# First stage of an attention and two-MoE kernel: the written-out order of its 1002 steps, and the engines of 168 of them, replaced

## The chip, the cores and the metric

The kernel runs on one core of a Trainium2 chip. The metric is device time in microseconds (us) of one launch. Engines are named as the profile names them: PE (TensorE matmul), PEld (TensorE weight load), DVE (VectorE), ACT (ScalarE), POOL (GpSimd), SP (SyncE, which here issues the DMAs of this stage). SBUF is the on-chip working memory and PSUM the memory that matmuls write.

## The reference

Attention over 2 batches, 8 heads, 768 positions, head size 64, each row seeing 8 global keys and the 96 last ones; then a dense mixture of 4 experts, weighted by given probabilities; then a mixture of 8 experts with a capacity of 192 tokens each, chosen by sorting all gate logits.

```python
scores = scale * q @ k.T + bias;  scores = where(keep, scores, -1e9)     # keep: global or local
a = exp(scores - max); a = a / (sum(a) + 1e-9);  x = a @ v               # (1536, 512) after reordering
out1 = sum_e p[:, e] * (relu(x @ w1[e]) @ w2[e])                         # 4 experts, 512 -> 1024 -> 512
out  = routed: relu(out1[mask] @ v1[e]) @ v2[e]                          # 8 experts, 192 tokens each
```

## The kernel before

Every float32 operand is split into a float16 high part and a float16 low part after scaling by a power of two, and each product is made of three float16 matmuls. So next to the matmuls there are many elementwise passes of 128 x 512: one that makes the high part (`hi`), one that subtracts it (`lo`), and so on.

The kernel has several stages. The change touches only the first one (`phase1`), which does the attention for 12 blocks of 128 rows, j = 0 to 11, and for each finished block the first MoE expert (e = 0). Later stages do experts 1 to 3, the routing, and the 8 routed experts; their code is the same in both kernels. The second stage begins with matmuls of expert 1, whose first weight matrix (weights 2) and second one (weights 3) are loaded and split near the end of stage one.

The steps of `phase1` are small closures with names, and a string `ORDER1` lists all 1002 of them in the order in which they are emitted. Each engine has one in-order queue, so the list fixes the order on every engine, on SP's DMA queue too. A token `name.j` is step `name` of block j (without `.j`: 0), and `/V`, `/A`, `/G` puts it on DVE, ACT or POOL; without a suffix it takes the default of `ENGINE`:

```python
ENGINE = dict(whi="G", hi="G", bias="G", keys="V", values="V", ph="G", pl="G", xhi="A", relu="A", hhi="V",
              hlo="G", add="A")
```

The steps of a block, with the line that the profile shows:

- `load` (three DMAs of q, k, v, L552), `sq` (sums of squares, ACT, L561), `run`, `total`, `scale` (power-of-two scales, a dozen tiny DVE instructions, L569 to L599).
- `hi0..2` (L544 on DVE, L540 on ACT, L542 on POOL) and `lo0..2` (DVE, L620: 128 x 512, reads two SBUF tensors); `T0`, `T1` (DMA transposes), `swap` (two DMAs).
- `keys`, `values`, `kglob`, `vglob` rescale the former block's keys and values; `bias` is two instructions, from bf16.
- `qk0..3` (PE, L695), `max0..3` (DVE, L706: reads PSUM and one SBUF tensor), `exp` (ACT, L715), `ph` (copy to f16, `/V /A /G`), `pl` (the rest: L730, DVE or POOL), `PT0`, `PT1` (DMA transposes), `pv` (PE, L753), `x` (three DVE instructions, L762 to L765).
- `norm` (ACT, L778), `rscale`, `xhi`, `xlo` (DVE, L791) and `xT` (DMA transpose, L770), which makes the block ready for the expert.
- `g00..g13` (8 steps of 12 matmuls, L834), `relu0/1`, `hhi0/1` (high part), `hlo0/1` (L1383, DVE or POOL), `y00..y07` (24 matmuls of 512 columns, L845), `add0`.

Weights k = 0 to 3: `wl0.k`, `wl1.k` (two DMAs of 1 MB, L372), `wsq` (ACT, L402), `wsum` (PE, L408), `wsc` (DVE), `whi0..7.k` (any engine), `wlo0..7.k` (DVE, L473). `wl0.3` may start when `wlo0.2` to `wlo3.2` have read their buffer, `wl1.3` after `wlo4.2` to `wlo7.2`. At the end of the old list SP finds `PT1.11`, `xT.10`, `wl0.3`, `xT.11`, `wl1.3` in this order. `check` makes sure that every step comes after those that it depends on.

Of the kernel before, what the change touches and what calls it, by code (L numbers as in the profile page):

```python
# [49 lines left out]
    max0.1 exp0.1 PT0 wlo6 qk1.1 max1.1 pl2 qk2.1 ph3 pl3 PT1 bias1.1 max2.1 qk3.1 sq0.3 max3.1 pv lo2.2 wsq1.1 x  # L50
    ph0.1 pl0.1 wsum.1 sq2.3 T1.2 norm exp1.1 exp2.1 wsc.1 keys.2/G run.3 ph1.1/A both ph2.1/A total.3 T0.2 bias0.2
    whi1.1 rscale scale.3 xhi/V kglob.2 values.1/G load.4 exp3.1 xlo sq1.4 swap.2 xT pl1.1 wlo1.1 PT0.1 hi2.3/V hi1.3
    qk0.2 max0.2 lo1.3 pl2.1 ph3.1/A whi5.1/A pl3.1 qk1.2 sq0.4 lo2.3 wlo4 whi2.1 hi0.3/A vglob.1 g00 pe0 sq2.4
    bias1.2/A exp0.2 max1.2 g01 whi4.1 lo0.3 g02 g03 PT1.1 g10 T1.3 run.4 ph0.2 total.4 T0.3 wlo2.1 g11 qk2.2 pv.1
    scale.4 whi7.1 max2.2 qk3.2 load.5 x.1 swap.3 exp1.2 exp2.2 hi1.4 hi0.4 relu0 keys.3 bias0.3 pl0.2/V max3.2 norm.1
    g12 ph1.2/A ph2.2/V hhi0/A rscale.1 g13 xhi.1 exp3.2 sq1.5 whi3.1 lo0.4 kglob.3 xlo.1 pl2.2 whi0.1 ph3.2 wlo5.1
    sq0.5 lo1.4 T0.4 pl1.2/V qk0.3 xT.1 pl3.2 qk1.3 sq2.5 max0.3 max1.3 relu1 T1.4 qk2.3 values.2 qk3.3 hi2.4/A g00.1
    g01.1 g02.1 wlo0.1 vglob.2 bias1.3/A wlo4.1 PT0.2 keys.4 hhi1/A PT1.2 exp0.3 bias0.4 exp1.3 g03.1 whi6.1 ph0.3/A
    g10.1 run.5 hlo0 swap.4 max2.3 total.5 scale.5 y00 g11.1 y01 hi1.5 pv.2 g12.1 pl0.3/V ph1.3/A hi0.5 hlo1/V lo2.4
    kglob.4 lo0.5 pl1.3/V relu0.1 wl0.2 exp2.3 y02 x.2 qk0.4 g13.1 max3.3 norm.2 bias1.4 ph2.3/V wlo3.1 rscale.2  # L60
    exp3.3 load.6 xhi.2 PT0.3 sq1.6 hi2.5/V max0.4 xlo.2 qk1.4 ph3.3 lo1.5 wlo6.1 y03 T0.5 xT.2 exp0.4 sq0.6 pl2.3
    sq2.6 y04 max1.4 y05 qk2.4 pl3.3 T1.5 max2.4 qk3.4 values.3/G exp1.4 ph0.4 y06 exp2.4 run.6 keys.5 total.6 vglob.3
    wlo7.1 max3.4 kglob.5 g00.2 bias0.5 g01.2 scale.6 y07 tiles.1 relu1.1/V ph1.4 pl0.4/V pl1.4 g02.2 hi1.6 hhi0.1/A
    swap.5 g03.2 pe0.1 exp3.4 PT1.3 hlo0.1 qk0.5 lo2.5 pv.3 g10.2 hi0.6/A x.3 g11.2 ph2.4/A pl2.4 g12.2 load.7 max0.5
    y00.1 lo0.6 ph3.4/V sq1.7 PT0.4 bias1.5 norm.3 T0.6 rscale.3 qk1.5 pl3.4/V bias0.6 xhi.3/G hhi1.1 exp0.5 max1.5
    hlo1.1 PT1.4 sq0.7 values.4/A sq2.7 g13.2 qk2.5 ph0.5 xlo.3 add0 vglob.4 max2.5 y01.1 lo1.6 y02.1 hi2.6/V run.7
    pe0.2 xT.3 y03.1 y04.1 pl0.5 qk3.5 y05.1 exp1.5 relu0.2/V y06.1 ph1.5 exp2.5 lo2.6 max3.5 swap.6 pv.4 T1.6 y07.1
    ph2.5/A g00.3 total.7 g01.3 x.4 g02.3 pl1.5 relu1.2 scale.7 tiles.2 exp3.5 ph3.5/A hhi0.2 hi1.7/V bias1.6 qk0.6
    pl2.5 g03.3 norm.4 hi0.7/A pl3.5 PT0.5 qk1.6 hlo0.2 rscale.4 g10.3 max0.6 load.8 xhi.4/V hi2.7 g11.3 g12.3 g13.3
    values.5/A y00.2 sq1.8 lo0.7 qk2.6 hhi1.2/A xlo.4 PT1.5 lo1.7 exp0.6 y01.2 relu0.3/V y02.2 sq0.8 max1.6 pe0.3  # L70
    y03.2 T0.7 bias0.7 hlo1.2 ph0.6 y04.2 xT.4 T1.7 sq2.8 y05.2 qk3.6 vglob.5 y06.2 exp1.6 pv.5 y07.2 ph1.6 tiles.3
    max2.6 exp2.6 run.8 lo2.7 keys.7/G relu1.3/V pl0.6/V hhi0.3 load.9 hlo0.3 g00.4 add0.1/V kglob.7 g01.4 g02.4 g03.4
    total.8 g10.4 y00.3 swap.7 hhi1.3/G relu0.4 hlo1.3 g11.4 max3.6 x.5 exp3.6 y01.3 norm.5 ph2.6/V y02.3 pl2.6
    ph3.6/A sq1.9 scale.8 hi1.8 g12.4 qk0.7 y03.3 sq0.9 hi0.8/V qk1.7 pl1.6 y04.3 pl3.6/V lo0.8 rscale.5 xhi.5 bias1.7
    max0.7 g13.4 sq2.9 xlo.5 wl1.2 PT0.6 bias0.8 hi2.8/V max1.7 lo1.8 qk2.7 PT1.6 pe0.4 y05.3 T0.8 xT.5 y06.3 exp0.7
    y07.3 tiles.4 ph0.7 exp1.7 hhi0.4/G qk3.7 hlo0.4 max2.7 pv.6 T1.8 add0.3/V exp2.7 ph1.7 swap.8 add0.2 relu1.4
    lo2.8 y00.4 load.10 max3.7 y01.4 x.6 ph2.7 y02.4 keys.8/A g00.5 g01.5 run.9 exp3.7 y03.4 pl2.7/V total.9 kglob.8
    ph3.7/A g02.5 pl0.7 scale.9 qk0.8 g03.5 max0.8 norm.6 qk1.8 pl1.7 hhi1.4/A rscale.6 sq1.10 PT0.7 bias1.8 pl3.7
    exp0.8 g10.5 hlo1.4 g11.5 hi1.9 values.7 hi0.9/V pe0.5 g12.5 ph0.8 y04.4 lo0.9 qk2.8 g13.5 vglob.7 bias0.9/A
    max1.8 y05.4 sq0.10 y06.4 lo1.9 xhi.6/V relu0.5/V hi2.9/A qk3.8 PT1.7 xlo.6 pl0.8 y07.4 tiles.5 sq2.10 T0.9 exp1.8  # L80
    hhi0.5/G hlo0.5/V pv.7 relu1.5 T1.9 y00.5 keys.9/A max2.8 y01.5 ph1.8 xT.6 exp2.8 run.10 y02.5 hhi1.5/G lo2.9
    hlo1.5 pl1.8 max3.8 y03.5 exp3.8 swap.9 x.7 norm.7 load.11 total.10 y04.5 PT0.8 y05.5 g00.6 ph2.8 ph3.8/A kglob.9
    pl2.8 scale.10 rscale.7 g01.6 y06.5 xhi.7/G qk0.9 pl3.8/V hi1.10/A g02.6 g03.6 max0.9 sq1.11 xlo.7 qk1.9 hi0.10/A
    y07.5 sq0.11 exp0.9 PT1.8 relu0.6/V max1.9 g10.6 tiles.6 hhi0.6/A bias1.9 pe0.6 qk2.9 exp1.9 values.8 xT.7
    bias0.10 lo0.10 g11.6 g12.6 g13.6 hlo0.6 add0.4 ph0.9/V T0.10 vglob.8 qk3.9 sq2.11 max2.9 lo1.10 y00.6 y01.6 pv.8
    g00.7 T1.10 relu1.6 g01.7 exp2.9 run.11 pl0.9 max3.9 hhi1.6/A g02.7 g03.7 swap.10 values.9 keys.10 x.8 exp3.9
    ph1.9 y02.6 pl1.9 ph2.9 kglob.10 total.11 g10.7 hlo1.6 PT0.9 g11.7 g12.7 scale.11 ph3.9/A norm.8 qk0.10 qk1.10
    y03.6 hi2.10/A rscale.8 pl2.9 g13.7 max0.10 pl3.9 qk2.10 hi1.11/A PT1.9 xhi.8 relu0.7 exp0.10 xlo.8 xT.8 bias1.10
    ph0.10 y04.6 y05.6 max1.10 vglob.9 max2.10 y06.6 hi0.11/V hi2.11/V exp1.10 y07.6 pv.9 exp2.10 ph1.10 lo0.11 qk3.10
    tiles.7 hhi0.7 T0.11 max3.10 g00.8 g01.8 relu1.7 lo2.10 lo2.11 lo1.11 pl0.10 ph2.10/A hlo0.7/V pe0.7 values.10/G  # L90
    g02.8 exp3.10 g03.8 hhi1.7 add0.6 g10.8 pl2.10 x.9 add0.5/V T1.11 ph3.10/V g11.8 relu0.8/V g12.8 y00.7 y01.7
    pl1.10 y02.7 hlo1.7 swap.11 close0 keys.11 bias0.11/A y03.7 kglob.11 gate3 y04.7 wsq0.2 y05.7 pe0.8 y06.7 norm.9
    y07.7 qk0.11 rscale.9 PT0.10 wsq1.2 qk1.11 g13.8 max0.11 tiles.8 hhi0.8/A pl3.10 relu1.8/V hlo0.8 max1.11 y00.8
    y01.8 vglob.10 qk2.11 PT1.10 xhi.9 xlo.9 y02.8 bias1.11 y03.8 pv.10 exp0.11 qk3.11 hhi1.8 max2.11 wsum.2 hlo1.8/V
# [1751 lines left out]
```

## Time and profile before

| what | value |
|---|---|
| runs | 895.56, 891.95, 895.22 us, median 895.22 |
| profiled execution | 895.84 us, span 894.1 us |
| mean granted TensorE clock | 0.962 |
| busy in the span | PE 755.8 us, DVE 645.1, ACT 528.1, POOL 334.4 |
| stage one | from the start to 256.46 us, where the first matmul of expert 1 starts |

A span is the time from the first to the last instruction; the profiled execution's own time is 1.7 us longer. A busy time is the sum of an engine's instruction times, without overlaps. An instruction that is held up inside the engine by another engine is busy too, for longer.

### The profile page before, as it was taken

The page shows a single profiled execution, that of the slowest core. Times are in us where ns is not written, and L with a number is a line of the kernel's source. Part 1 is how long each engine was busy: PE and PEld are TensorE (multiplying, and loading weights), DVE is VectorE, ACT ScalarE, POOL GpSimd, SP SyncE. Part 2 cuts the span into 40 slices and gives each one's busy share as a digit, 9 for nine tenths or more (in the row PEclk, how much of TensorE's full clock was granted, in tenths as well). Part 3 has the DMA queues.
Part 4 walks back from the last instruction along what each step waited for, and adds up shares of the span by engine and source line. Part 5 has one row for each costly group of instructions (what it writes and reads, how often), then busy time and mean ns, then how long its engine had stood idle before and what let it go on. Part 6 is the DMA issues. An engine that isn't in the chain of part 4 may idle for free.

```text
span 894.1 us, 19304 instructions
## 1 busy us (share of the span) xinstructions
PE 755.8 (85%) x7539; PEld 544.6 (61%) x7539; DVE 645.1 (72%) x1710; ACT 528.1 (59%) x1046; POOL 334.4 (37%) x403
## 2 busy tenths in 40 slices
...
GB/s 232 217 177 184 178 188 212 151 112 139 154 142 0 108 81 1 95 31 89 1 26 12 14 25 14 36 2 1 59 213 84 131 139 347 247 277 321 193 34 39
DMA packets 196860, 105.20 MB, mean 118 GB/s; under 512 B 167585, under 2 KB 167585, under 8 KB 196769
## 3 DMA queue, kind: packets, MB, share of 16 engines
...
q0 software_dynamic: 2048, 6.34, 3.0%
q8 instruction: 59, 0.97, 0.5%
...
## 4 chain that ended last, share of the span: by engine, by line
PE 41%; DVE 25%; issue 12%; DMA 9%; ACT 7%; POOL 4%; SPq 1%; POOLq 0%; DVEq 0%; ACTq 0%
PE pH L834 16%; PE pY L845 14%; DVE C L967 3%; PE pR L834 2%; PE pY L1012 2%; ACT junk L402 2%; DVE jk L970 2%; DMA xt<-xs 2%; DVE t L706 2%; DMA xk<-in_k_dram 2%; PE pH L1255 2%; DMA xg<-g 2%; DVE w L473 1%; PE pR L1275 1%; POOL out_dram L1291 1%
## 5 line engine op out<-in xcount | busy, mean ns | idle before, releaser
L834 PE MATMUL pH<-xT,w 128*128 128x128 f16 (+2 forms) x2304 | 238.7, 263 | 10.7 <-DMA xT<-xs 9.2
L834 PEld LDWEIGHTS <-w 128*128 128x128 f16 x2592 | 209.0, 100 | 61.8 <-DMA xT<-xs 7.1
L845 PE MATMUL pY<-w,hh 128*128 128x512 f16 x544 | 162.3, 380 | 3.7 <-DVE y L544 1.3
L808 ACT ACTIVATE H<-pH 128x512 f32<-128x512 f32 (+1 forms) x94 | 52.8, 564 | 100.6 <-PE pH L834 75.8
L845 PE MATMUL pY<-w,hl 128*128 128x512 f16 x272 | 103.4, 380 | 4.2 <-POOL hl L1383 3.1
L980 ACT ACTIVATE Cj<-C 128x128 bf16<-128x128 bf16 (+11 forms) x88 | 75.3, 856 | 43.1 <-DVE C L967 42.1
L542 POOL TENSOR_SCALAR hh<-H 128x512 f16<-128x512 f32 x55 | 36.6, 665 | 134.3 <-ACT H L808 123.8
L845 PEld LDWEIGHTS <-hh 128*128 128x128 f16 x544 | 49.9, 98 | 52.9 <-issue 2.6
L1255 PEld LDWEIGHTS <-w 128*128 128x128 f16 x768 | 65.5, 100 | 23.4 <-DMA xg<-g 18.5
L432 DVE SCALAR_TENSOR_TENSOR w<-raw,wsr,w 128x1024 f16<-128x1024 f32 x52 | 65.2, 1278 | 6.3 <-ACT w L540 6.3
L1275 PE MATMUL pR<-hh,w 128*128 128x192 f16 x512 | 67.1, 249 | 0.0
L1255 PE MATMUL pH<-xg,w 128*128 128x192 f16 x528 | 49.8, 254 | 20.2 <-DMA xg<-g 18.3
L803 DVE TENSOR_TENSOR hl<-H,hh 128x384 f16<-128x384 f32 (+1 forms) x56 | 34.6, 617 | 44.2 <-POOL hh L542 43.1
L967 DVE TENSOR_SCALAR C<-LR,Lg 128x1024 bf16<-128x1024 f32 (+7 forms) x88 | 64.1, 729 | 3.1 <-PE pw L986 1.7
L1275 PEld LDWEIGHTS <-w 128*128 128x128 f16 x768 | 64.7, 99 | 2.3 <-issue 2.0
L1275 PE MATMUL pR<-hl,w 128*128 128x192 f16 x256 | 63.8, 249 | 0.0
L1012 PE MATMUL pY<-w,xT 128*128 128x512 f16 x192 | 61.6, 396 | 0.0
L402 ACT ACTIVATE w<-raw 128x2048 f16<-128x2048 f32 x18 | 34.3, 1905 | 42.1 <-PE pY L845 23.4
L715 ACT ACTIVATE t<-t,mx,ec 128x256 f32<-128x256 f32 (+1 forms) x96 | 55.2, 576 | 2.9
L540 ACT ACTIVATE w<-raw,wsr 128x1024 f16<-128x1024 f32 (+1 forms) x49 | 50.7, 1053 | 6.5 <-DVE wsr L302 6.5
L852 DVE SCALAR_TENSOR_TENSOR y<-pY,pe,y 128x512 f32<-128x512 f32 x22 | 16.5, 748 | 51.6 <-PE pY L845 47.0
L695 PE MATMUL pS<-kT,qT 128*128 128x128 f16 x176 | 29.4, 245 | 25.9 <-DVE mx L706 9.9
...
## 6 DMA issues: line engine op xcount, KB each, us to landing
...
pt<-pp SPq DMA_TRANSPOSE x24, 4.9
```

The costliest lines, as they stand in the source:

```text
L402: A.activation(x, s.raws[k, q][0], AF.Square, accum_out=J["ss"][:, q:q + 1])
L432: V.scalar_tensor_tensor(l, r[:, d2], sc, h, op0=OP.mult, op1=OP.subtract)
L540: s.nc.scalar.activation(out, x, AF.Copy, scale=sc)
L715: s.nc.scalar.activation(t[:, o + hh], t[:, o + hh], AF.Exp, bias=mx[:, 1, hh:hh + 1], scale=e[:, 0:1], accum_out=s.SU[j][:, 2 * g + hh:2 ...
L808: s.nc.scalar.activation(H, ps, AF.Relu, scale=HS)
L834: nc.tensor.matmul(o[f], w[:, d, 128 * (f0 + f):128 * (f0 + f) + 128], x[:, :, c], start=(d == 0 and i == 0), stop=(d == 3 and i == 2))
L845: nc.tensor.matmul(py, l[:, f], w[:, f], start=(f == 0 and i == 0), stop=(f == 7 and i == 2))
L967: V.tensor_scalar(C[:, 8 * i:8 * i + n], x[:, :n, e], l, None, op0=OP.is_ge)
L980: s.nc.scalar.activation(x, C, AF.Copy, accum_out=s.AC[j][:, 1, e:e + 1])
L1012: nc.tensor.matmul(py, a[:, f], w[:, f], start=(n == 0), stop=(n == 23))
L1255: nc.tensor.matmul(ps[0][:, f % 2], w[:, d, 128 * f:128 * f + 128], xg[:, :, c], start=(k == 0), stop=(k == 11))
L1275: nc.tensor.matmul(ps[0][:, d % 2], w[:, f, 128 * d:128 * d + 128], h[:, f], start=(k == 0), stop=(k == 23))
```

## The change

Only `ORDER1` changes: the same 1002 steps, in another order, with 168 of them on another engine. No function changes. How many steps of each kind lie on an engine, before and after:

| step | DVE | ACT | POOL |
|---|---|---|---|
| whi | 4, 8 | 11, 10 | 17, 14 |
| hi | 10, 4 | 12, 13 | 14, 19 |
| bias | 0, 1 | 5, 11 | 19, 12 |
| keys | 5, 6 | 3, 0 | 2, 4 |
| values | 4, 4 | 3, 1 | 3, 5 |
| ph | 8, 11 | 17, 18 | 23, 19 |
| pl | 16, 16 | 0, 0 | 32, 32 |
| xhi | 4, 3 | 5, 6 | 3, 3 |
| relu | 12, 10 | 12, 14 | 0, 0 |
| hhi | 9, 7 | 8, 9 | 7, 8 |
| hlo | 7, 12 | 0, 0 | 17, 12 |
| add | 5, 5 | 7, 7 | 0, 0 |

The start and the end of the two lists (the middle is of the same make):

```diff
-    load sq1 sq0 sq2 wl0 run wl1 route total scale wsq0 hi1/V load.1 hi0/A wsq1 lo1 lo0 hi2 sq1.1 lo2 wsum wsc gate0
-    whi5 sq0.1 whi1/A whi3/V sq2.1 gate1 whi2/V wlo5 gate2 T0 T1 whi4/A run.1 load.2 total.1 wlo3 whi7/A swap tiles
...
-    ph0.11/A exp1.11 y04.8 exp2.11 pl0.11/V ph1.11 max3.11 xT.9 y05.8 ph2.11/V pl1.11/V y06.8 pl2.11/V y07.8 g00.9
-    g01.9 x.10 exp3.11 ph3.11/A pl3.11/V norm.10 tiles.9 add0.7/V g02.9 g03.9 g10.9 g11.9 g12.9 relu0.9/V PT0.11
-    rscale.10 hhi0.9/G hlo0.9/V pe0.9 g13.9 xhi.10/G y00.9 relu1.9/V values.11/A xlo.10 vglob.11 hhi1.9 wsc.2 y01.9
-    y02.9 PT1.11 hlo1.9 y03.9 whi2.2 pv.11 y04.9 whi7.2/V y05.9 whi6.2 whi0.2/A whi1.2 y06.9 xT.10 whi3.2/A whi5.2
-    y07.9 g00.10 x.11 whi4.2 wlo0.2 norm.11 wlo6.2 tiles.10 g01.10 pe0.10 rscale.11 xhi.11/V g02.10 xlo.11 g03.10
-    relu0.10/V g10.10 g11.10 add0.9 hhi0.10/G wlo5.2 g12.10 add0.8/V wlo1.2 wlo3.2 wlo2.2 g13.10 wlo7.2 wlo4.2 close1
-    wl0.3 relu1.10/V xT.11 wsq0.3 hlo0.10 wl1.3 y00.10 y01.10 y02.10 y03.10 g00.11 g01.11 g02.11 wsq1.3 hhi1.10 g03.11
-    g10.11 hlo1.10/V y04.10 wsum.3 y05.10 wsc.3 y06.10 y07.10 g11.11 g12.11 g13.11 relu0.11 whi2.3 tiles.11 wlo2.3
...
+    load wl0 wl1 sq1 sq0 sq2 run total scale hi1/V gate0 load.1 wsq0 wsq1 hi0/V hi2 wsum gate1 lo1 lo0 lo2 sq1.1 T0 T1
+    sq0.1 sq2.1 wsc wl0.1 gate2 whi7/V whi5/V swap wlo7 bias0 whi6/V run.1 total.1 whi2/A qk0 wlo6 scale.1 hi1.1/V
...
+    qk2.11 max2.11 xT.9 hlo1.8 exp0.11 y03.8 exp1.11 pv.10 x.10 y04.8 whi6.2/V g00.9 whi0.2/V qk3.11 values.11/G g01.9
+    norm.10 max3.11 g02.9 g03.9 y05.8 g10.9 rscale.10 whi4.2 exp2.11 xhi.10 ph0.11 y06.8 vglob.11 g11.9 ph2.11/A
+    relu0.9 whi7.2/A pe0.9 xlo.10 y07.8 ph1.11 tiles.9 exp3.11 xT.10 ph3.11/A whi2.2/A pl0.11/V add0.7/V hhi0.9
+    hlo0.9/V g12.9 g13.9 y00.9 relu1.9 y01.9 g00.10 pe0.10 pl1.11 hhi1.9 g01.10 hlo1.9/V y02.9 pl2.11/V y03.9 y04.9
+    PT0.11 y05.9 y06.9 y07.9 pl3.11 wlo6.2 wlo0.2 PT1.11 whi5.2/A g02.10 add0.8 whi3.2/V wlo5.2 g03.10 wlo2.2 add0.9
+    wlo4.2 tiles.10 wlo1.2 pv.11 wlo7.2 g10.10 close1 wlo3.2 g11.10 g12.10 relu0.10/V hhi0.10/G x.11 g13.10 norm.11
+    wl0.3 hlo0.10 rscale.11 relu1.10 wsq0.3 wl1.3 xhi.11/V xlo.11 hhi1.10/G hlo1.10/V xT.11 y00.10 wsq1.3 pe0.11
+    y01.10 y02.10 y03.10 y04.10 y05.10 y06.10 y07.10 wsum.3 wsc.3 g00.11 g01.11 whi3.3 g02.11 whi4.3/V whi5.3 g03.11
...
```

In the middle, SP's queue differs in one thing of size: `wl0.2` stands behind `swap.4` in the old list and behind `swap.10` in the new one, `wl1.2` behind `swap.7` and now behind `swap.11`.

## Rows read from the trace of the kernel before

**Rows 1.** Busy time by stretch (us, then each engine's busy us and count, clock, DMA).

```profile
16.24:215.70 199.46, 146.47 (x1956) 114.06 (x1956) 186.45 (x541) 156.48 (x413) 132.12 (x140) 0.97 0.93 175
215.70:224.90 9.20, 9.20 (x137) 6.98 (x135) 8.02 (x21) 2.62 (x5) 4.88 (x6) 1.00 0.86 125
224.90:256.46 31.56, 24.75 (x248) 17.90 (x247) 18.21 (x35) 9.41 (x14) 8.87 (x10) 0.89 0.44 143
...
100.00:215.70 115.70, 104.68 (x1446) 78.63 (x1444) 110.92 (x319) 92.48 (x240) 79.34 (x83) 1.00 0.87 162
...
241.10:246.50 5.40, 5.40 (x61) 5.40 (x62) 0.00 (x0) 3.68 (x6) 0.00 (x0) 0.60 1.05 386
```

**Rows 2.** DVE's instructions by line in stage one: ns minimum/median/maximum, first and last start.

```profile
L620 DVE SCALAR_TENSOR_TENSOR kn<-xk,asr,kn x12: 739/1184/1665, 10.0 to 197.9; 128x512 f16<-128x512 f32 x12
...
L574 DVE CAST ssb<-ssr x11: 171/173/1152, 18.0 to 180.6; 128x3 bf16<-128x3 f32 x11
...
L706 DVE CUSTOM_DVE_ANT_0 t<-pS,t x96: 271/414/425, 25.4 to 212.1; 128x256 f32<-128x256 f32 x80, 128x128 f32<-128x128 f32 x16
...
L544 DVE TENSOR_SCALAR hh<-H x8: 408/417/836, 107.3 to 236.0; 128x512 f16<-128x512 f32 x8
...
L1383 DVE TENSOR_TENSOR hl<-H,hh x6: 675/691/1092, 82.0 to 236.4; 128x512 f16<-128x512 f32 x6
```

**Rows 3.** DVE in order of time, 89 to 95 us (start, us).

```profile
91.03 1.64 DVE L620 SCALAR_TENSOR_TENSOR kn<-xk,asr,kn 128x512 f16<-128x512 f32 x1
92.60 1.60 DVE L473 SCALAR_TENSOR_TENSOR w<-y,wsr,w 128x512 f16<-128x512 f32 x1
```

**Rows 4.** POOL in order of time, the same stretch.

```profile
89.41 2.72 POOL L730 TENSOR_TENSOR pp<-t,pp 128x512 f16<-128x512 f32 x2
92.11 1.55 POOL L542 TENSOR_SCALAR vs<-vs,ratio 128x1024 f16<-128x1024 f16 x1
```

**Rows 5.** POOL's instructions by line in stage one: ns minimum/median/maximum.

```profile
L542 POOL TENSOR_SCALAR t<-bias,ec x38: 477/695/1452, 22.4 to 207.5; 128x512 f32<-128x512 bf16 x32, 128x256 f32<-128x256 bf16 x6
...
L542 POOL TENSOR_SCALAR kn<-xk,asr x6: 695/699/859, 51.7 to 154.7; 128x512 f16<-128x512 f32 x6
...
L542 POOL TENSOR_SCALAR vs<-vs,ratio x3: 1116/1117/1553, 47.2 to 194.8; 128x1024 f16<-128x1024 f16 x3
...
L1383 POOL TENSOR_TENSOR hl<-H,hh x16: 1151/1160/1585, 74.7 to 231.0; 128x512 f16<-128x512 f32 x16
```

**Rows 6.** DVE in order of time, 224 to 235 us.

```profile
224.21 0.69 DVE L765 TENSOR_TENSOR x<-pO,rs 128x512 f32<-128x512 f32 x1
224.82 2.00 DVE L473 SCALAR_TENSOR_TENSOR w<-raw,wsr,w 128x512 f16<-128x512 f32 x2
...
228.39 0.75 DVE L791 SCALAR_TENSOR_TENSOR xs<-x,rsr,xs 128x512 f16<-128x512 f32 x1
...
230.98 4.34 DVE L473 SCALAR_TENSOR_TENSOR w<-raw,wsr,w 128x512 f16<-128x512 f32 x5
```

**Rows 7.** What SP's queue waited for, 221 to 236 us (us, times, longest).

```profile
SPq L372 <- DVE w L473: 11.8, 1, 11.8
```

**Rows 8.** The chain that ended last, 222 to 262 us (start, us).

```profile
234.60 6.45 DMA xT<-xs
241.10 5.56 PE pH L834 x60
...
251.28 5.18 PE pY L845 x24
```

**Rows 9.** PE in order of time: block 10's g, undisturbed.

```profile
226.00 5.52 PE L834 MATMUL pH<-xT,w 128*128 128x128 f16 x96
```

**Rows 10.** Line 770: issue to landing of the xT transposes, all 12.

```profile
DMA to landing us min/median/max: 3.2/3.6/4.1
```

**Rows 11.** ACT in order of time: the two squares of weights 3.

```profile
240.10 1.91 ACT L402 ACTIVATE w<-raw 128x2048 f16<-128x2048 f32 x1 [13.21 <-DMA raw<-in_moe_w_dram]
...
243.80 1.91 ACT L402 ACTIVATE w<-raw 128x2048 f16<-128x2048 f32 x1 [1.69 <-DMA raw<-in_moe_w_dram]
```

More of the change, by code (lines that the diff above doesn't have):

```diff
@@ L50 @@
[L50 to L94, printed above, removed]
@@ new lines @@
+    qk1.1 lo1.2 wsum.1 wsc.1 exp0.1 qk2.1 T0.2 max1.1 qk3.1 sq1.3 ph3 sq0.3 max2.1 pl3 T1.2 whi6.1 PT1 ph0.1/V both
+    sq2.3 run.3 lo2.2 total.3 max3.1 scale.3 exp1.1 pv whi0.1 whi2.1 exp2.1 bias0.2/A pl0.1 ph1.1 hi1.3 keys.2 probs
+    swap.2 tiles kglob.2 x ph2.1/A lo1.3 exp3.1 ph3.1/A qk0.2 hi0.3/V load.4 max0.2 norm pl1.1 qk1.2 pl2.1 lo0.3
+    bias1.2 consts sq1.4 qk2.2 rscale hi2.3 pl3.1/V max1.2 values.1/G PT0.1 exp0.2 wlo2.1 qk3.2 T1.3 sq0.4 sq2.4
+    whi7.1/A max2.2 xhi/G run.4 xlo ph0.2 exp1.2 total.4 T0.3 whi1.1 exp2.2 ph1.2/A scale.4 lo2.3 vglob.1 PT1.1
@@ new lines @@
+    hi1.4/A max3.2 pv.1 xT hi2.4/A wlo6.1 swap.3 keys.3/G pe0 pl0.2 hi0.4 ph2.2/A bias0.3/A g00 load.5 kglob.3 x.1
+    norm.1 lo1.4 pl1.2 PT0.2 wlo1.1 g01 qk0.3 rscale.1 qk1.3 exp3.2 lo0.4 whi5.1 sq1.5 ph3.2/A g02 values.2 max0.3
+    pl2.2 g03 vglob.2 xhi.1/V sq0.5 pl3.2 g10 g11 g12 qk2.3 sq2.5 max1.3 T0.4 wlo0.1 whi4.1 qk3.3 run.5 exp0.3 xlo.1
+    bias1.3/A lo2.4 total.5 T1.4 ph0.3 g13 scale.5 bias0.4 keys.4 exp1.3 max2.3 PT1.2 hi1.5/A max3.3 hi0.5 pl0.3 pv.2
+    ph1.3/A lo1.5 kglob.4 swap.4 relu1 qk0.4 exp2.3 xT.1 load.6 qk1.4 relu0/V exp3.3 max0.4 g00.1 lo0.5 g01.1 g02.1
```

47 lines of the change are left out of this document (41 added, 6 removed).

## The prediction

> **What bounds the kernel now.** I read the busy shares by slice first (VectorE is at nine tenths or more through most of the first quarter), then the busy time by stretch, then DVE's instructions by line, then the chain that ended last over the end of the stage, and last SP's waits there. Stage one falls into three stretches [rows 1]: A, from 16.24 us, when the first weight scale is known, to 215.70, when DVE has finished the last `pl` (`pl3.11`); B, to 224.90, when `x.11` ends; C, to 256.46, when expert 1 starts.
>
> In A the DVE is busy 186.5 of 199.5 us: it sets the pace. But much of this is not its own work. A `lo` takes 0.74 us at the least and 1.18 in the median, up to 1.67; a copy of three numbers takes 0.17 or up to 1.15; `max`, with one of its tensors in PSUM, never varies (0.425 at the most for the wide form) [rows 2]. Two slow ones in a row, 1.64 and 1.60 us, stand beside POOL instructions that follow each other without a gap and are long too [rows 3, 4]: the two engines take turns. From the start of one to that of the next these DVE instructions are 1.57 us apart, the length of one POOL instruction and one `lo` together.
>
> How much of A is such waiting: I took each form of DVE instruction at its least duration ([rows 2] has the first and four more of some sixty), less the 0.08 us by which it begins before the one before it ends (91.03 plus 1.64 against 92.60 [rows 3]), times its number in the list up to `pl3.11`. That gives 140 us, of which 4 lie before A. So 186.5 - 136 = 50 us of A are waits for POOL. POOL's own work up to there, counted in the same way ([rows 5] has four of its forms), is 113 us: it costs the DVE 50/113 = 0.44 us per us.
>
> In C the engines wait for one thing. `xlo.11` ends at 229.14 [rows 6], but its transpose is issued at 234.60, because SP's queue stands at `wl0.3`, whose buffer the `wlo.2` steps on DVE still read: SP waits 11.8 us for them [rows 7], the last row of them starts at 230.98 [rows 6]. The transpose then takes 6.45 us [rows 8] against 3.6 in the median and 4.1 for the slowest of the twelve that the line's view tells of [rows 10]; the load of 1 MB issued just before it is the only thing new beside it. PE stands still until 241.10, and after that idle time its granted clock is 0.60 [rows 1], between its two levels: 60 matmuls take the time to 246.5, 5.4 us, where 96 took 5.52 at full clock [rows 9]. That is about 2 us lost.
>
> **The change, part by part.** No instruction is added or taken away; the sums are changes of engine and place.
>
> *A, DVE's own work.* Counting tokens up to `pl3.11`, DVE has 22 instructions more in the new list: six `hlo` (0.68 each, 4.1), one `xlo` (0.74), one `add` (0.74), four more of the short scaling kind (eleven for `whi`, `ph`, `bias`, `keys` and `hhi` more, seven for `hi` and `xhi` fewer; 0.42 each [rows 2], 1.7), nine tiny ones of 0.15 (by the cast of three numbers [rows 2]) and a `vglob` (together 1.8). That is 9.1, less 0.08 of overlap for the thirteen larger ones: plus 8. Most were in stretch B before; they come earlier.
>
> *A, POOL's work.* Fourteen `bias` instructions fewer (0.695, -9.3, some narrower), four `hlo` fewer (1.15, -4.6), four `ph` fewer (0.62 by the narrow `hhi` kind, -2.4); five `hi` more (+3.5), two `keys` and two `values` more (1.12 each, +4.5), two small ones (+1.3) [rows 5]. Sum -7: 106 us.
>
> *A, the turns.* At the old rate the new list has 106 x 0.44 = 47 us of waiting, 3 less. That is the upper end, if the new layout does not place POOL's work better. The lower end: the DVE's forms that never waited (`max`, `x`, the reads of PSUM in `relu` and `add`) hold about 50 us in A (`max` alone 80 x 0.41 and 16 x 0.28, 37 [rows 2]; `x`, `relu` and `add` some 20 pieces of the 0.69 of `x` [rows 6]), its idle time is 13, and some 0.13 us of each of 131 POOL instructions hide in the turn itself (start to start 1.57 us [rows 3], where a 0.66 `lo` and a 1.12 `values` would make 1.78 in a row); if POOL filled all of that, 106 - 50 - 13 - 17 = 26 us remain. Both queues are in order and wait for other engines too, so a plan is met only in part; I take 42, a quarter of the way down. A comes out at +8 - 8 = 0, with ends of +5 and -16.
>
> The Trainium skill ("SBUF — State Buffer", "Who interferes with whom") has a rule that speaks against a gain here: the ports that DVE and GpSimd share are an exclusive lock, and the one that comes second waits out the first one's whole instruction. Taken strictly nothing hides in a turn, the 17 us fall away, the least waiting is 106 - 50 - 13 = 43 us, A is +1 at the best and the sum 886. The turns of 1.57 us where the two instructions are 1.78 in a row show that here a part does hide.
>
> *A, PE's cover.* Before the end of `pv.11` the new list has PE do 5.2 us more (four `y` steps at 0.65, four `g` steps at 0.67 [rows 8, 9]). Between 100 and 215.7 us PE has 115.7 - 104.7 = 11 us idle [rows 1] and B has none. So 0 for A and B together needs half of that idle time gone, and A and B can't shrink by more than 6 however well the turns go, unless PE is ahead at 100 us already. It is not: the first `xT` comes about 7 us of DVE work later than before, and the PE work in front of `pv.3` is 3 us less.
>
> *B.* Its length is that of a transpose (`PT1.11`) and `pv.11`; in the new list the eight `wlo.2` (0.66 each from start to start, 5.3 us) lie in it where the work moved to A stood. 0. If that cover were gone, 5.3.
>
> *C.* Now SP has `wl0.3`, `wl1.3`, `xT.11` in this order, and all of `wlo.2` ends before `x.11`. Counting from the end of `x.11` (t): `wl0.3` and `wl1.3` are issued about t - 2. In the old tail the first load was squared 5.9 us after its issue (234.2 to 240.1), the second 9.6 us after the first's issue (243.8) [rows 11]; so the second is squared from t + 7.6 and `wsum.3`, which stands in PE's queue before `g00.11` in the new list, can run at t + 7.6 + 2.1 + 0.4 = t + 10. `xlo.11` ends at t + 3 (it was 4.2 with two `wlo` of 2.00 between [rows 6]); its transpose has two loads before it, lands with the second or 2 us later, and so at t + 8 to t + 10. I take `g00.11` at t + 10 (it was t + 16.2). Then 5.4 us of `g` [rows 9] and 5.2 of `y` [rows 8]. PE has `g10..g13.10` and all of `y.10`, 7.9 us, to fill from `pv.11` to t + 6.5: it idles some 3.5 us where it was 6.6, and I charge half of the clock loss, 1. C lasts 10 + 5.4 + 5.2 + 1 = 21.6 us where it was 31.6: -10. Ends: -12.5 (no clock loss, loads as fast as the first) and -6 (the second load lands 4 us later).
>
> *Moved past queues.* `wl0.2` and `wl1.2` leave the middle for the last blocks; there they go before `PT`, `T` and `xT` of blocks 9 to 11. I cost this at 0, hidden by the PE backlog of that stretch (9.2 of 9.2 busy [rows 1]); a rival below has its price. The later stages keep their code, and their first stretch is PE's, so what stage one gives passes on whole.
>
> Sum: 0 + 0 - 10. Against the profiled execution's 895.84 us this is 885.8; the median of the runs is 0.6 lower, so **885**.
>
> **The rivals.** 0.5% of the time, 4.5 us, is about what a measurement can tell here.
>
> *The turns are as frequent as before* (the change doesn't do what it says). A is +5, C still -10: 890. For it: the list orders each engine but not the engines against each other, and the start of POOL's instructions hangs on ACT and DMA. Against: POOL has 7 us less to do.
>
> *The turns fall much, and PE is the cap.* A and B together -6, C -10: 879. For it: POOL's `bias` work goes to ACT, which has 43 us idle in A [rows 1]. Against: PE would have to run A's last 115 us without a gap.
>
> *Slower: the weight loads move into DMA's busy part.* The DMA engines are at 0.93 in A [rows 1], and one load of 1 MB before a transpose cost 2.9 us (6.45 against 3.6). Two loads now stand in front of blocks 10 and 11, with `wsq1.2` close behind `wl1.2` in ACT's queue, in front of `exp.11`. If the transposes of two blocks (`T`, `PT`) each lose 3 us and ACT waits 4 for the load, A is +5 + 6 + 4 = +15, and with the second load late C gives only 6: +9, 904. It decides from the point where PE has no backlog in blocks 10 and 11. Against: PE was busy for all of B [rows 1], so it had a backlog there.
>
> *The tail gives half.* `wsum.3` in front of `g00.11` waits for a late second load, C -6, and A +2 from the PE work ahead: 891.
>
> **How the numbers follow.** Forecast 0.38 (own range 881 to 889), same turns 0.24, PE cap 0.16, slower 0.11, half tail 0.11. Faster by over 0.5% (under 890.7): 0.38 + 0.16 and two thirds of the second, 0.16: 0.70. Slower: 0.11. Same: 0.19. The range takes in the cap, and the slower case in part: 874 to 899.
>
> **What would show it.** DVE's `lo` median near 0.75 to 1.0 instead of 1.18, and POOL's busy time down by over 7 us. A over by 214 to 218 us on DVE. No SP wait of 10 us on `wlo` before `xT.11`; PE's gap before `g.11` under 4 us; expert 1 starting near 246. Wrong would be: the same medians with PE's gaps longer in the last blocks (turns), an ACT wait on a raw load of several us before `exp.11` (slower rival), or a start of expert 1 after 252.

## The result, and the profile after

The changed kernel takes **880.5 us** (median of 4 runs, 878.84 to 883.16) against 895.39 us before (4 runs, 891.95 to 896.15). The ratio of the runs is 0.9855, with a 95% interval of 0.9818 to 0.9893 (the two medians alone make 0.983): faster by 1.5%. The profiled execution took 880.59 us, with a span of 878.8 us.

Busy time by stretch after (stretch, length, then busy us and count of PE, PEld, DVE, ACT and POOL, granted clock, DMA share, GB/s). Stretch A ends with the later of the last two `pl`; that is now `pl2.11`, on DVE (`pl3.11`, on POOL, ends at 210.1).

```profile
15.60:211.75 196.15, 151.44 (x2052) 120.20 (x2052) 186.94 (x564) 164.17 (x431) 120.22 (x126) 0.98 0.98 181
211.75:219.18 7.43, 7.43 (x109) 5.31 (x107) 7.27 (x14) 0.69 (x1) 0.96 (x2) 1.00 0.63 133
219.18:241.00 21.82, 19.31 (x181) 13.50 (x178) 9.03 (x20) 8.08 (x12) 7.42 (x9) 0.92 0.65 194
100.00:211.75 111.75, 104.77 (x1431) 79.58 (x1429) 107.98 (x324) 93.55 (x247) 68.91 (x70) 1.00 0.91 170
```

Beside [rows 1]: A and B together end at 219.18 instead of 224.90 (-5.7), C lasts 21.82 us instead of 31.40 (-9.6), and expert 1 starts 15.3 us earlier. Both are read from the first matmul of expert 1, which before starts at 256.30; the 256.46 above is where the matmul ahead of it ends:

```profile
256.30 1.89 PE L834 MATMUL pH<-xT,w 128*128 128x512 f16 x8
```

This lead stays to the end: the span is 15.3 us shorter.

DVE's `lo`, its copies of three numbers and the steps beside them, by line (ns minimum/median/maximum, first and last start):

```profile
L620 DVE SCALAR_TENSOR_TENSOR kn<-xk,asr,kn x12: 732/743/1153, 10.6 to 182.1; 128x512 f16<-128x512 f32 x12
...
L574 DVE CAST ssb<-ssr x11: 170/361/1107, 17.7 to 168.5; 128x3 bf16<-128x3 f32 x11
```

The median `lo` of k went from 1184 to 743 ns [rows 2], which looks as if the turns were gone. They are not: the median copy of three numbers, 173 ns before, is 361 ns now. All 36 `lo` together (of k, v and q) took 40.5 us before (15.4, 14.4 and 10.7) and take 32.4 now (9.9, 12.3 and 10.2), where 26.5 would be without a wait. So the `lo` wait 8 us less, which is the whole fall in the table below; what all other forms wait, taken together, is what it was. Summed as in the prediction (each form at its least, up to the last `pl`), DVE's time from 15.5 us on is:

| us | before | after |
|---|---|---|
| DVE's own work | 135.7 | 143.5 |
| waits for POOL inside DVE's instructions | 51.5 | 43.5 |
| DVE idle | 13.1 | 9.3 |
| POOL's own work | 112.8 | 106.0 |
| end of the last `pl` | 215.78 | 211.75 |

DVE's own work and its waits cancel (+7.8 and -8.0). That A ends 4.0 us earlier is its idle time (-3.8).

The end of the stage, as the chain that ended last shows it (start, us, what):

```profile
217.47 8.93 DMA raw<-in_moe_w_dram
...
226.43 2.01 ACT w L402 x2
...
228.81 0.16 PE pq L408
228.97 7.01 PE pH L834 x96
235.98 5.18 PE pY L845 x24
```

SP no longer stands 11.8 us at `wl0.3` [rows 7]. Both loads are issued before `x.11` ends, and what holds `g00.11` is `wsum.3`, which waits for the second load and its square. PE idles 2.5 us there, and the 96 matmuls of `g.11` then take 7.0 us where 5.52 is undisturbed [rows 9].

### The profile page after: what moved, and what is told of

Its sections match the earlier page's. It is cut to its first block, busy times and chain, and to the rows that moved or that the text cites. A ratio compares the mean times of both kernels' runs of the same rounds, so it can differ in the third digit from the quotient of the medians.

```text
span 878.8 us, 19320 instructions
## 1 busy us (share of the span) xinstructions
PE 751.9 (86%) x7539; PEld 543.6 (62%) x7539; DVE 634.9 (72%) x1714; ACT 530.8 (60%) x1058; POOL 320.4 (36%) x387
## 4 chain that ended last, share of the span: by engine, by line
PE 42%; DVE 26%; issue 12%; DMA 10%; ACT 6%; POOL 3%; SPq 0%; POOLq 0%; DVEq 0%; ACTq 0%
PE pH L834 17%; PE pY L845 13%; DVE C L967 3%; PE pR L834 2%; DMA xt<-xs 2%; DVE t L706 2%; PE pH L1255 2%; DVE jk L970 2%; PE pR L1275 2%; DMA rows<-xs 2%; DMA xg<-g 2%; ACT junk L402 1%; DMA qT<-qT 1%; ACT w L540 1%; POOL out_dram L1291 1%
## 5 line engine op out<-in xcount | busy, mean ns | idle before, releaser
L834 PEld LDWEIGHTS <-w 128*128 128x128 f16 x2592 | 208.0, 99 | 59.6 <-issue 7.7
L834 PE MATMUL pH<-xT,w 128*128 128x128 f16 (+2 forms) x2304 | 238.9, 262 | 1.6 <-DMA xT<-xs 1.6
L845 PEld LDWEIGHTS <-hl 128*128 128x128 f16 x272 | 26.6, 98 | 33.4 <-POOL hl L1383 1.2
```

The source lines that it names most:

```text
L834: nc.tensor.matmul(o[f], w[:, d, 128 * (f0 + f):128 * (f0 + f) + 128], x[:, :, c], start=(d == 0 and i == 0), stop=(d == 3 and i == 2))
L845: nc.tensor.matmul(py, l[:, f], w[:, f], start=(f == 0 and i == 0), stop=(f == 7 and i == 2))
```

## The experiments

Twelve kernels, in four questions. In the four kernels `old_seq_new_eng`, `new_seq_old_eng`, `old_tail` and `new_tail` the list has one line less, so their line numbers are one lower (L833 for L834).

### What sets the pace of stretch A

`less_PE` has two matmuls instead of three in each `y` step, `less_DVE` zeros for `lo`, `less_POOL` zeros for POOL's `pl` (one execution of each):

```diff
-            for i, (l, w) in enumerate(((hh, W[2]), (hh, W[3]), (hl, W[2]))):
+            for i, (l, w) in enumerate(((hh, W[2]), (hh, W[3]), (hl, W[2]))[:3 - first]):
```
```diff
-        V.scalar_tensor_tensor(lo, x, s.sc[j][0][:, c:c + 1], hi, op0=OP.mult, op1=OP.subtract)
+        V.memset(lo, 0.0)
```
```diff
-        (G if eng == "G" else V).tensor_sub(pl[:, x], t[:, x], ph[:, x])
+        G.memset(pl[:, x], 0.0) if eng == "G" else V.tensor_sub(pl[:, x], t[:, x], ph[:, x])
```

> The changed kernel, with the third of the three matmuls of each y step of stage one left out (the product of the hidden rest with the high part of the second weights), so PE has 64 instructions of 512 columns, some 18 us, less to do up to the end of block 10; DVE, ACT and POOL do the same work. Theory (PE is what ends stretch A: it serves 22 to 23 us of every 25 and blocks 10 and 11 run behind it): the last pl ends 4 to 8 us earlier, at 202 to 206 us instead of 210.1. Rival (DVE and POOL, who take turns, set the pace on their own): the last pl ends within 2 us of 210.1. The total falls in any case, since the y steps of blocks 10 and 11 behind it are shorter by 1.7 us each, and so is not what is read.

> The changed kernel, with the 36 lo steps of q, k and v replaced by a DVE instruction that only writes zeros (the low parts of q, k and v are left out). DVE has 36 times some 0.4 us, 14 us, less work of its own up to the last pl, and with it fewer turns against POOL; PE does the same work. Theory (PE ends stretch A): the last pl ends 0 to 4 us earlier, 206 to 210. Rival (DVE and POOL set the pace): 10 us or more earlier, at 200 or before.

> The changed kernel with the 32 pl steps of POOL replaced by a POOL instruction that only writes zeros (the low parts of these probabilities are left out): some 0.8 us less for each, 26 us less POOL work; DVE's and PE's work is the same. Theory (DVE waits for POOL by turns, at 0.42 us per us of POOL work, and PE is the next bound, 6 us away): the waits of DVE's instructions for POOL fall from 45 to some 34 us, x.11 ends 4 to 7 us earlier, 212 to 215. Rival (the waits within DVE's instructions come from something else): they stay within 3 us of 45 and x.11 within 2 us of 219.2.

The windows of the three, from 100 us to the last `pl` or a little past it, `less_PE` first:

```profile
100.00:213.55 113.55, 95.86 (x1358) 77.13 (x1356) 106.75 (x323) 93.02 (x245) 67.15 (x70) 0.95 0.96 169
```
```profile
100.00:205.70 105.70, 102.52 (x1399) 77.79 (x1398) 92.94 (x309) 90.33 (x239) 62.03 (x68) 1.00 0.94 177
```
```profile
100.00:203.59 103.59, 101.64 (x1401) 77.88 (x1399) 97.65 (x316) 91.28 (x240) 51.20 (x67) 1.00 1.00 177
```

With 9 us less PE work in this window, the last `pl` ends at 213.55, 1.8 us later than in the changed kernel (`wsum_mid` below, the same list up to there, has it at 213.22, so runs differ by that much). So PE does not set the pace: the rival was right, my theory wrong. With less DVE work `x.11` ends at 213.01 instead of 219.18 (-6.2), and with less POOL work at 211.01 (-8.2, where 4 to 7 were expected). In both PE is then busy for 97 and 98% of the window. DVE and POOL set the pace, and PE, by its busy share, is the next bound, 6 to 8 us below; no run took work from two engines at once. In `less_DVE` neither expectation held: `pl3.11`, whose end the 210.1 is, ends at 203.96, 6.2 us earlier, between the theory's 4 and the rival's 10.

In `less_POOL` the waits inside DVE's instructions fall from 43.5 to 30.2 us (some 34 were expected), and the 36 `lo` take 28.0 us together instead of 32.4:

```profile
L620 DVE SCALAR_TENSOR_TENSOR kn<-xk,asr,kn x12: 734/742/953, 10.6 to 173.9; 128x512 f16<-128x512 f32 x12
...
L730 POOL MEMSET pp<- x32: 309/522/527, 32.5 to 196.4; 128x512 f16 x27, 128x256 f16 x5
```

So most of these waits hang on POOL's reads; not all do, as three copies of three numbers still took 0.45, 0.45 and 0.90 us with only such zeros beside them. The 32 `pl` held 34.5 us at their least (27 of 1.157 and 5 narrow ones of 0.66): 13.3/34.5 = 0.39 us of waiting per us of POOL work, near the 0.41 of the whole (43.5/106). The Trainium skill ("SBUF — State Buffer", "Who interferes with whom") has a DVE instruction with two SBUF inputs contend with a GpSimd instruction that reads SBUF, and not with one that only writes; these rows agree.

The turns by themselves are in a kernel of its own:

> A kernel of its own that measures the turns (it computes nothing of the reference). Eight stretches: 16 DVE lo alone; 8 POOL copies of 128x512 (the hi form) alone; 8 POOL pl alone; 24 lo beside 16 POOL hi; 24 lo beside 12 POOL pl; 30 DVE copies of 128x512 to f16 beside 12 pl; 20 DVE reads of PSUM (the relu form) beside 12 pl; 60 DVE casts of 3 columns beside 12 pl. Theory (the engines take turns at SBUF, one instruction each): one lo and one POOL instruction pass per turn, from start to start 1.2 us beside hi (0.66 + 0.69 less some 0.15) and 1.7 beside pl; the copies wait as the lo do; the reads of PSUM keep their 0.61 us, and pl beside them its length alone; of the casts one in each turn waits for about 1 us. Rival (both engines run at once and share the rate): lo and POOL's instructions are all longer by a steady share, under 1.4 times, and the casts by nothing.

Its instructions did not run in the written order: the stretches are mixed, so `lo` beside `hi` alone was not measured. What stands side by side can be read. DVE, then POOL, in order of time (start, us):

```profile
12.97 1.70 DVE L41 SCALAR_TENSOR_TENSOR lo<-x,sc,hi 128x512 f16<-128x512 f32 x1
14.60 0.68 DVE L47 TENSOR_SCALAR H<-pH 128x512 f32<-128x512 f32 x1
...
64.33 0.74 DVE L41 SCALAR_TENSOR_TENSOR lo<-x,sc,hi 128x512 f16<-128x512 f32 x1
65.00 1.11 DVE L50 CAST ssb<-ssr 128x3 bf16<-128x3 f32 x1
66.02 0.74 DVE L41 SCALAR_TENSOR_TENSOR lo<-x,sc,hi 128x512 f16<-128x512 f32 x1
...
125.39 0.17 DVE L50 CAST ssb<-ssr 128x3 bf16<-128x3 f32 x1
125.51 0.75 DVE L41 SCALAR_TENSOR_TENSOR lo<-x,sc,hi 128x512 f16<-128x512 f32 x1
...
126.30 0.75 DVE L41 SCALAR_TENSOR_TENSOR lo<-x,sc,hi 128x512 f16<-128x512 f32 x1
```
```profile
12.98 1.15 POOL L56 TENSOR_TENSOR pl<-t,ph 128x512 f16<-128x512 f32 x1
14.11 1.13 POOL L53 TENSOR_SCALAR kn<-x,sc 128x512 f16<-128x512 f32 x1
...
48.69 1.15 POOL L56 TENSOR_TENSOR pl<-t,ph 128x512 f16<-128x512 f32 x1
49.82 0.69 POOL L53 TENSOR_SCALAR kn<-x,sc 128x512 f16<-128x512 f32 x1
...
62.93 18.66 POOL L56 TENSOR_TENSOR pl<-t,ph 128x512 f16<-128x512 f32 x12
```

Beside a stream of `pl` one `lo` and one cast pass every 1.69 us (64.33 to 66.02), which is a `pl` (1.13) and a `lo` (0.66) less 0.10; with POOL silent the pair takes 0.79 (125.51 to 126.30). (The strict lock that the prediction weighed, from the same section of the Trainium skill, would make 1.79; the measured 1.69 decides.) Which DVE instruction is held hangs on the order: here the cast of three numbers pays 0.95 us and the `lo` nothing, and at 12.97 the `lo` pays 0.96. Turns, one instruction each, are what the theory said. The reads of PSUM keep their length, whatever POOL does beside them, as the line of all 20 shows (minimum/median/maximum):

```profile
L47 DVE TENSOR_SCALAR H<-pH x20: 672/678/691, 1.9 to 36.0; 128x512 f32<-128x512 f32 x20
```

### Sequence or engines

The old sequence with the new engines, and the new sequence with the old engines (each token keeps its place and takes the other list's suffix):

```diff
-    whi5 sq0.1 whi1/A whi3/V sq2.1 gate1 whi2/V wlo5 gate2 T0 T1 whi4/A run.1 load.2 total.1 wlo3 whi7/A swap tiles
+    whi5/V sq0.1 whi1 whi3/A sq2.1 gate1 whi2/A wlo5 gate2 T0 T1 whi4/A run.1 load.2 total.1 wlo3 whi7/V swap tiles
...
-    sq0.1 sq2.1 wsc wl0.1 gate2 whi7/V whi5/V swap wlo7 bias0 whi6/V run.1 total.1 whi2/A qk0 wlo6 scale.1 hi1.1/V
+    sq0.1 sq2.1 wsc wl0.1 gate2 whi7/A whi5 swap wlo7 bias0/A whi6/A run.1 total.1 whi2/V qk0 wlo6 scale.1 hi1.1/A
```

> The old sequence of steps with the new list's engines for the 168 moved steps. Theory (most of the gain is the sequence of the last two blocks, and a third of it the run up to pl3.11): up to pl3.11 DVE has 2 us more of its own work, POOL 8 less, at the old 0.45 us of waiting per us of POOL that is -2 in A; the tail keeps the SP wait before xT.11, C stays 31 us; time 892 to 895. Rival (the gain comes from taking work off POOL): A shrinks by 5 or more, time 888 to 890.

> The new sequence with the old engines. Theory: up to pl3.11 DVE has 5 us more of its own work than before and POOL 5 more, so A is 3 to 8 us longer than before, but C keeps most of its gain (-8 to -10): 888 to 893. Rival (the turns are laid out for these engines, so a wrong assignment breaks them): A more than 10 longer, 896 or more. Rival (sequence alone is the cause): 881.

Measured: 914.7 us (ratio 1.022, 1.018 to 1.026) and 897.7 us (1.005, 1.003 to 1.006). Both are slower than before. Neither expectation of the first held; of the second the first rival came (897.7, and A ends at 228.74, 13 us later). (Of the second the profile shows its fastest run, 892.13 us.) The waits for POOL are 44.0 us, as little as in the changed kernel, and 47.5, half way back to 51.5; what grew is DVE's idle time, to 36.4 and 23.3 us. Of the first, what DVE waited for in A (us, times, longest):

```profile
DVE t L705 <- PE pS L695: 7.3, 4, 4.1
DVE hl L1382 <- POOL hh L541: 4.0, 2, 2.1
DVE hl L1382 <- ACT hh L539: 3.5, 2, 2.9
DVE rse L296 <- ACT xs L777: 2.9, 4, 1.8
```

Each engine runs its steps in the order of the list. By these lines a step that was put on another engine at its old place waits there for work that isn't ready (`hlo` on DVE for `hhi` on POOL or ACT), and holds up what stands behind it. So the gain can't be shared out between engines and sequence; each half alone is a loss. C alone is short with the new sequence, whatever the engines: 18.9 us in the second kernel.

### The loads of weights 2

```diff
-    ph1.3/A lo1.5 kglob.4 swap.4 relu1 qk0.4 exp2.3 xT.1 load.6 qk1.4 relu0/V exp3.3 max0.4 g00.1 lo0.5 g01.1 g02.1
+    ph1.3/A lo1.5 kglob.4 swap.4 wl0.2 relu1 qk0.4 exp2.3 xT.1 load.6 qk1.4 relu0/V exp3.3 max0.4 g00.1 lo0.5 g01.1 g02.1
...
-    kglob.10 g01.7 swap.10 g02.7 pe0.7 x.8 pl1.9/V qk0.10 wl0.2 lo2.10 add0.5 hlo1.6 qk1.10 pl2.9/V exp3.9 ph3.9/A
+    kglob.10 g01.7 swap.10 g02.7 pe0.7 x.8 pl1.9/V qk0.10 lo2.10 add0.5 hlo1.6 qk1.10 pl2.9/V exp3.9 ph3.9/A
```

That is `wl_early` (the list is written here without its new line breaks), with `wl1.2` behind `swap.7` in the same way; in `wl_behind` they stand behind `load.6` and `load.9`; in `old_wl_late` the old list has them behind `swap.10` and `swap.11`.

> The changed kernel with the two loads of weights 2 back at their old places in SP's queue (wl0.2 behind swap.4, wl1.2 behind swap.7 instead of swap.10 and swap.11). Theory (the late loads cost nothing, PE's backlog hides them): 880 to 881.5, x.11 within 1.5 us of 219.2. Rival (the late loads hold up the transposes of blocks 10 and 11): 2 to 6 us faster, 875 to 878, x.11 at 213 to 217. Third (in the middle they cost more than at the end, since the DMA engines are full there): slower by over 2 us.

> The changed kernel with the loads of weights 2 in the middle, but each right behind the load of a block's q, k and v (wl0.2 behind load.6, wl1.2 behind load.9) and not in front of it. Theory (what an early load of 1 MB costs is the wait for the q, k and v queued behind it): the steps of 2.8 and 2.0 us at blocks 6 and 9 go, x.11 within 2 us of 219.2, 880 to 882. Rival (any 1 MB in the middle costs 2 to 3 us, then by the PT transposes behind it): x.11 at 223 to 226, 884 to 887.

> The kernel before with two steps moved in its list: wl0.2 from behind swap.4 to behind swap.10 and wl1.2 from behind swap.7 to behind swap.11, their places in the new list. The new list with the loads at the old places was 4 to 6 us slower than as it is, by a wait of ACT's squares for the k that is loaded behind the 1 MB load. Theory (the gain of stretches A and B comes from the late loads, whatever the rest of the list): 3 to 6 us faster than before, 888 to 891, x.11 at 219 to 222 instead of 224.9. Rival (in the old list the loads cost nothing, as no wait of ACT for them shows there; the gain of A and B needs the new sequence): within 2 us of before, 892 to 895; a wait of ACT for the late loads in front of exp.11 can make it slower.

`wl_early` took 886.6 us (10 runs, ratio 0.9921, 0.9887 to 0.9954): slower than the changed kernel, the third case. In its trace A ends at 218.03 and `x.11` at 225.44, which is 6.3 us later than in the changed kernel and within 0.6 us of before. Most of the delay comes in steps, 2.8 us at block 6 and 2.0 at block 9. (These are single profiles: `wsum_mid` below, with the changed kernel's list up to there, has `x.11` 1.5 us later than that.) The first step, on ACT (in brackets the idle time in front), `wl_early` and then the changed kernel:

```profile
85.42 0.63 ACT L561 ACTIVATE vs<-xk 128x512 f16<-128x512 f32 x1 [3.03 <-DMA xk<-in_k_dram]
```
```profile
82.34 0.61 ACT L561 ACTIVATE vs<-xk 128x512 f16<-128x512 f32 x1
```

The next block's k is queued behind 1 MB (issued at 74.68), its square waits, and the scale and DVE with it. That shows as idle time of DVE, 14.7 us of A against 9.2 (202.43 - 187.69 here, 196.15 - 186.94 in the changed kernel):

```profile
15.60:218.03 202.43, 154.97 (x2059) 121.93 (x2059) 187.69 (x567) 165.29 (x436) 120.01 (x126) 0.97 0.97 176
```

Put behind that load (`wl_behind`, 885.8 us, 0.9898, 0.9855 to 0.9941, `x.11` at 227.38 in the profile of its slowest run), the 1 MB meets the next transposes instead. SP there:

```profile
78.81 1.38 SPq L372 DMA_DIRECT2D raw<-in_moe_w_dram  x1
80.30 6.93 SPq L738 DMA_TRANSPOSE pt<-pp  x1
```

So in the middle of the new list 1 MB costs 2 to 3 us at either place: the rival. At the end of the new list it costs nothing that shows: SP has 2.4 and 1.5 us to wait anyway between each load and what follows, and the squares wait for neither (on SP, then on ACT):

```profile
169.76 1.37 SPq L372 DMA_DIRECT2D raw<-in_moe_w_dram  x1
173.57 5.53 SPq L738 DMA_TRANSPOSE pt<-pp  x2
...
187.92 0.58 SPq L372 DMA_DIRECT2D raw<-in_moe_w_dram  x1
189.97 6.36 SPq L738 DMA_TRANSPOSE pt<-pp  x2
```
```profile
193.62 1.90 ACT L402 ACTIVATE w<-raw 128x2048 f16<-128x2048 f32 x1
...
195.52 1.89 ACT L402 ACTIVATE w<-raw 128x2048 f16<-128x2048 f32 x1
```

In the old list the same move is a loss: 906.9 us (1.0153, 1.0109 to 1.0198), `x.11` 10.4 us later. Neither time came, only the mishap named beside the rival. But the rival's reason holds: with no such load before 184.50, the old list is no faster up to block 8. The `x` of blocks 3 to 8 in the kernel before, then in `old_wl_late` (the last two times are the first and the last start):

```profile
L765 DVE TENSOR_TENSOR x<-pO,rs x6: 691/692/692, 103.9 to 184.2; 128x512 f32<-128x512 f32 x6
```
```profile
L765 DVE TENSOR_TENSOR x<-pO,rs x6: 690/692/693, 104.0 to 184.6; 128x512 f32<-128x512 f32 x6
```

So in the old list the loads cost nothing in the middle. At their late places the transposes follow the loads at once, ACT waits 5.5 us for the second one in front of `exp.11`, and DVE 4.7 us for scores that PE can't start (SP, ACT, DVE):

```profile
184.50 0.58 SPq L372 DMA_DIRECT2D raw<-in_moe_w_dram  x1
185.19 8.66 SPq L738 DMA_TRANSPOSE pt<-pp  x2
```
```profile
211.00 1.91 ACT L402 ACTIVATE w<-raw 128x2048 f16<-128x2048 f32 x1 [5.53 <-DMA raw<-in_moe_w_dram]
```
```profile
198.50 0.42 DVE L706 CUSTOM_DVE_ANT_0 t<-pS,t 128x256 f32<-128x256 f32 x1 [4.72 <-PE pS L696]
```

### The tail

`old_tail` and `new_tail` put `xT.11` in front of both loads of weights 3 on SP, and the rest of weights 3 behind the hidden part of block 11 (the diff is that of the old list); `wsum_mid` moves the sum alone.

```diff
-    wl0.3 relu1.10/V xT.11 wsq0.3 hlo0.10 wl1.3 y00.10 y01.10 y02.10 y03.10 g00.11 g01.11 g02.11 wsq1.3 hhi1.10 g03.11
+    relu1.10/V xT.11 wl0.3 wl1.3 hlo0.10 y00.10 y01.10 y02.10 y03.10 g00.11 g01.11 g02.11 hhi1.10 g03.11
...
+    y00.11 hhi1.11 y01.11 y02.11 hlo1.11/V wsq0.3 wsq1.3 y03.11 y04.11 y05.11 y06.11 y07.11 wsum.3 wsc.3 whi2.3 wlo2.3
```

In `wsum_mid`:

```diff
-    y01.10 y02.10 y03.10 y04.10 y05.10 y06.10 y07.10 wsum.3 wsc.3 g00.11 g01.11 whi3.3 g02.11 whi4.3/V whi5.3 g03.11
+    y01.10 y02.10 y03.10 y04.10 y05.10 y06.10 y07.10 g00.11 g01.11 g02.11 g03.11 wsum.3 wsc.3 whi3.3 whi4.3/V whi5.3
```

> The old list with the end alone rearranged: on SP xT.11 ahead of wl0.3, and wsq, wsum, wsc, whi and wlo of weights 3 behind block 11's hlo1 or y07. Theory (the tail's wait on SP and the clock loss after it cost 7 to 9 us): xT.11 issued at 229, no PE gap before g.11, expert 1 starts at 248 instead of 256.5, time 886 to 889. Rival (xT.11 was hidden by other PE waits, or weights 3 late stop expert 1): 893 to 896.

> The new list with the same rearrangement: xT.11 ahead of wl0.3 and wl1.3, weights 3 behind block 11. Theory: PE's gap of 2.5 us before g.11 and the slow clock after it (96 matmuls in 7.0 us where 5.4 are normal) go, expert 1 starts at 237 instead of 241, time 876 to 878. Rival (weights 3 come too late and the stage after pays it back, or DVE and POOL, which now split weights 3 beside expert 1, delay its hidden parts): 880 to 883.

> The changed kernel with one edit: the sum of weights 3 on PE (wsum.3, wsc.3) stands behind g03.11 in the list and no longer in front of g00.11. In the changed kernel PE stood 2.5 us before this sum and g.11 then took 7.0 us where 5.4 is normal, while the transfers of xT.11 seem over by 225.6 us, before y07.10 ends at 226.3. Theory (the sum alone held PE up, and nothing behind it needs the weights sooner): g.11 follows y07.10 without a gap at about 226.3, takes 5.5 us, expert 1 starts near 237 (4 us earlier), and as the sum itself still runs at 229.1, the splits of weights 3 are not later: the time falls by 3 to 4 us, 876.5 to 877.5. Rival (the splits of weights 3 end too late for an earlier expert 1, as in the rearranged tail of before): expert 1 starts 4 us earlier and its second to eighth group wait for ACT, the time falls by under 2 us, 879 to 881.

`old_tail`: 888.5 us (0.9943, 0.9919 to 0.9967), as expected. Expert 1 starts 9.2 us earlier than before, but 4.4 us of this are lost again by its eighth group. `new_tail`: 881.5 us (0.9866, 0.9847 to 0.9886), the same as the changed kernel and in the rival's range. Expert 1 starts at 236.45, 4.55 us earlier, and by its eighth group all of that is given back; the span ends 1.7 us shorter. What PE waited for then, and why: the eight `wlo.3` in a row on DVE in front of the hidden part of expert 1, and ACT at the next raw load (waits view of PE; DVE; ACT):

```profile
PE pH L833 <- ACT H L807: 4.6, 3, 3.2
```
```profile
239.71 6.95 DVE L472 SCALAR_TENSOR_TENSOR w<-raw,wsr,w 128x512 f16<-128x512 f32 x8 [1.93 <-POOL w L541]
```
```profile
251.57 1.91 ACT L401 ACTIVATE w<-raw 128x2048 f16<-128x2048 f32 x1 [3.49 <-DMA raw<-in_moe_w_dram]
```

`wsum_mid`: 880.7 us (0.9839, 0.9761 to 0.9917), in the rival's range but not by its mechanism: expert 1 starts at 243.31, no earlier. The gap before `g.11` is 0.9 us, and PE then stands 2.2 us before `y.11` instead, for the `hlo` on POOL behind the `whi.3`, which hang on the same sum:

```profile
PE pY L845 <- POOL hl L1383: 2.2, 1, 2.2
PE pH L834 <- DMA xT<-xs: 0.9, 1, 0.9
```

So the rest of the tail is a chain (load, square, sum, split) that shows up wherever it is put. No version here beats the changed kernel measurably.

## Why the prediction was right, and where it was not

885 was forecast and 880.5 came, inside the range and 0.5 us under the forecast's own range. The tail was right in cause and size. Stretches A and B were forecast at 0 and gave 5.7. Point by point:

- *DVE's own work, +8*: +7.8. Right.
- *The turns, 50 to 42 us*: 51.5 to 43.5. The size was right, and so was the "quarter of the way": at the old rate of 0.46 the 106 us of POOL work would have cost 48. What hides in a turn was read loosely: 1.57 us is not the length of the two instructions together, which the prediction itself puts at 1.78; 0.21 are hidden there and 0.13 were used, and beside the stream of `pl` 0.10 are. That moves only the lower end, which was not reached. The sign that I named, the median of `lo`, overstates the fall, since the other forms wait as much as before.
- *A comes out at 0, and "moved past queues ... I cost this at 0"*: this is the step that failed. Own work and waits cancel as said. The sum left DVE's idle time at 13 us and the moved loads at nothing; the idle time fell by 3.8 us and B by 1.8. The loads decide it. With them at the old places the new list ends A 2.2 us later than before and A and B together 0.5 us later, which is the forecast; with the loads late it is -5.7. So in the new list the place of the loads is worth 6 us. The old kernel did not pay these 6 us: its list is no faster up to block 8 without the loads (`old_wl_late`). The gain in A and B needs the new sequence and the late loads together. C gave 3 of it back (18.87 us in `wl_early`: the second load of weights 3 was squared 1.3 us sooner after its issue, and `g.11` ran at full clock). By the medians the whole move is worth 6 us, by the profiles 4.
- *PE's cover, A and B can't shrink by more than 6*: wrong. With the same PE work, `x.11` ends 11.9 us before that of the old kernel in `less_DVE` and 13.9 in `less_POOL`. What failed is "it is not": PE is ahead at 100 us. From the first scale to there the new list has 621 of its matmuls done, 46.7 us of work, the old one 510 and 41.8 (the first line less the last, in the rows after and in [rows 1]). The rival built on this bound, 879, is nearest to the result in its number by luck: the bound was not reached, and in `less_PE` less PE work gained nothing.
- *B, 0*: 7.43 instead of 9.20 us. Part of the same 5.7.
- *C, -10*: -9.6. The gap was 2.5 us and not 3.5, the clock loss 1.6 and not 1, and the sum was ready at 9.6 us after `x.11` where 10 was said.
- *What would show it*: A ends at 211.75, 2 us ahead of the 214 to 218 named, and expert 1 starts at 241 instead of 246. Both come of the 5.7 us above. The rest came.
- *The slower rival* did not come in the new list; its mechanism, transposes behind 1 MB and ACT waiting in front of `exp.11`, is what `old_wl_late` shows, at +10 us.

What stays open: why the new list has no slack for the loads in its middle where the old one has, and which of DVE's waits the late loads save it (its idle time is 9.3 us where the old list has 13.1). No run has the new list with no such load at all.
